# Sliding-window attention and a gated two-layer product in one program: the first batch's second half of keys and queries loaded ahead of the first layer's weights

## The chip, the cores and the metric

One core of a Trainium2 chip runs the whole program. It has five engines that run their own instruction streams in order and meet at semaphores: TensorE (PE; its weight loads are listed as PEld), VectorE (DVE), ScalarE (ACT), GpSimd (POOL) and SyncE (SP). Loads from memory are issued by POOL, since they change the type on the way (float32 in memory, 16-bit types on the chip). The metric is the device time of one execution in microseconds (us), lower is better, given as the median of several runs. Three runs of the kernel before took 290.44, 291.09 and 289.84 us.

## The reference

Two stages follow each other. First comes attention with a window of 32 positions to each side, over 8 batches, 8 heads, 576 positions and 64 channels:

```python
scores = scale * np.matmul(q, k.transpose(0, 1, 3, 2))
mask = np.abs(pos[:, None] - pos[None, :]) <= window      # window = 32
scores = np.where(mask, scores, -1000000000.0)
attn = np.exp(scores - np.max(scores, axis=-1, keepdims=True))
attn = attn / (np.sum(attn, axis=-1, keepdims=True) + 1e-09)
attn_out = np.matmul(attn, v)
```

Its output, with the heads side by side, is x (4608 tokens of 512 channels). Then come two matrix products with an activation between them:

```python
h = x @ w_in                                   # 512 -> 2048
g = h * (1.0 / (1.0 + np.exp(-1.702 * h)))
out = g @ w_out                                # 2048 -> 512
```

## The kernel before

The tokens are cut into 36 units of 128 rows (shifted by 32 rows, so that a unit's window needs its own keys and 64 of the next unit's) and into 9 tiles of 512 rows, four units each. For each unit `scores` (L238) multiplies keys and queries on PE and ACT takes the exponent; `band` (L258) multiplies by the mask on DVE; `values` (L266) multiplies by the values on PE; `norm` (L284) divides on DVE; `x_T` or `x_T2` (L298, L313) transposes the result on PE, and a copy puts it where layer one reads it. `values` needs the unit's values `ve` and a copy `vo` that is shifted by 64 rows: `odd_v(u)` (L201) copies the upper half of `ve[u]` and the lower half of `ve[u + 1]`, so it needs the loads of both.

Layer one of tile 0 is plain: `layer1_plain(0, d, half, bank)` (L378) makes two blocks of 128 features for 256 tokens with eight matrix products, and ACT applies the activation. `d` from 0 to 7 runs over the features; `d` 0 and 1 need the first quarter of w_in (`load_w1(0)`), 2 and 3 the second, and so on; `half` 0 needs units 0 and 1, `half` 1 units 2 and 3. The later tiles use a scheme with sums of blocks of w_in (`w1_sums`, L327), of w_out and of x. Layer two takes w_out in quarters (`load_w2`).

`opening` (L562) holds everything that this change touches. It is an order written out by hand, and each engine runs its share of it in this order. The staging of the first batch's keys and queries comes in two parts (`load_first`, L137, and `T_first`, L157, which transposes on PE and copies with two engines); the next tile's in one each (`load_four`, `T_four`, L173 and L181). `keep_busy` (L553) runs matrix products whose result nobody reads. Eight PSUM banks are handed out by name: A, C, B, E, LA, LB and "t", which is two. A step that takes a bank waits until the last reader of that bank is done.

POOL issues the loads one after another, in the order in which they stand. They share eight completion semaphores in turn, so a load can only be issued once the load eight places before it has landed. In the opening this is the order: first keys and queries part 0, values 0, 1, 2, first quarter of w_in, the mask, keys and queries part 1, second quarter of w_in, values 3 and 4, third quarter, the tile's keys and queries, fourth quarter, values 5 and 6, first quarter of w_out, values 7 and 8, the other quarters of w_out, and then what `fetch` brings for the later units. Unit 4's values come as two halves of 64 rows in any case, since a batch ends in the middle of it.

Of the kernel before, what the change touches and what calls it, by code (L numbers as in the profile page):

```python
# [26 lines left out]
class _Kernel:  # L27
# [166 lines left out]
    def load_v(self, u):  # L194
        if u >= self.NU:
            return
        t = self.ve[u % 9]
        for off, b, s, n in self.pieces(128 * u, 128):
            self.nc.gpsimd.dma_start(t[off:off + n, :, :self.D], self.v[b, :, s:s + n, :].rearrange("h s d -> s h d"))  # L199

    def odd_v(self, u, eng):  # L201

        vo = self.vo[u % 5]
        nxt = self.v_first if u == self.NU - 1 else self.ve[(u + 1) % 9][0:64]

        def words(ap):
            return ap.rearrange("p h d -> p (h d)").bitcast(I32)

        eng.tensor_copy(words(vo[64:128]), words(self.ve[u % 9][64:128]))  # L209
        eng.tensor_copy(words(vo[0:64]), words(nxt))  # L210
# [351 lines left out]
    def opening(self):  # L562

        nc, dve, act, pool = self.nc, self.nc.vector, self.nc.scalar, self.nc.gpsimd
        self.setup()
        dve.memset(self.idle, 0.0)
        dve.memset(self.spark, 0.0)
        for t in self.ve:
            dve.memset(t[:, :, self.D:], 1.0)
        self.load_first("k", 0)  # L570
        self.load_first("q", 0)
        make_identity(nc, self.ident)
        act.activation(self.spark, self.spark, AF.Exp)
        for u in (0, 1, 2):
            self.load_v(u)
        self.load_w1(0)
        self.setup_mask()
        self.load_first("k", 1)
        self.load_first("q", 1)
        self.cut_mask()  # L580
        self.load_w1(1)
        self.load_v(3)
        self.load_v(4)
        self.load_w1(2)
        self.load_four("k")
        self.load_four("q")
        self.load_w1(3)
        dve.tensor_copy(self.identh, self.ident)
        self.keep_busy(20, "E")
        self.T_first("k", 0, "AC", (dve, act))  # L590
        self.keep_busy(6, "E")
        self.T_first("q", 0, ("LA", "LB"), (dve, act))
        self.keep_busy(4, "E")
        for u in (5, 6):
            self.load_v(u)
        self.load_w2(0)
        for u in (7, 8):
            self.load_v(u)
        for c in (1, 2, 3):
            self.load_w2(c)  # L600
        self.load_kq("k", 8)
        self.scores(0, "t")
        self.scores(1, "AC")
        self.odd_v(0, dve)
        self.odd_v(1, dve)
        self.keep_busy(10, "E")
        self.band(0)
        self.band(1)
        self.values(0, "t")
        self.values(1, "AC")  # L610
        self.norm(0)
        self.norm(1)
        self.keep_busy(6, "E")
        self.x_T(0, "LA", act)
        self.keep_busy(4, "E")
        self.x_T(1, "LB", act)
        self.T_first("k", 1, "AC", (dve, dve))
        h, n, gelus = [], [0], []

        def l1(half, *ds):  # L620
            for d in ds:
                self.layer1_plain(0, d, half, h[n[0] % len(h)])
                n[0] += 1

        self.layer1_plain(0, 0, 0, "B", gelus)
        self.T_first("q", 1, ("LA", "LB"), (dve, act))
        self.layer1_plain(0, 1, 0, "E", gelus)
        self.odd_v(2, dve)
        self.odd_v(3, dve)
        h[:] = ["LB", "B", "E"]  # L630
        self.scores(2, "t")
        self.scores(3, "AC")
        self.layer1_plain(0, 2, 0, "LA", gelus)
        self.layer1_plain(0, 3, 0, "LB", gelus)
        self.do(gelus)
        self.band(2)
        self.band(3)
        self.values(2, "t")
        self.norm(2)
        self.values(3, "AC")  # L640
        self.norm(3)
        self.x_T2(2, "A", dve)
        l1(0, 4)
        dve.tensor_copy(self.k_first, self.kT[0][:, :, 0:64])
        dve.tensor_copy(self.v_first, self.ve[0][0:64])
        for u in (8, 9, 10, 11):
            self.fetch(u)
        l1(1, 0, 1)
        halo = self.kT[4]
        self.T_four("k", "AC", (dve, dve))  # L650
        dve.tensor_copy(self.kT[4][:, :, 0:64], halo)
        l1(1, 2, 3)
        l1(0, 5)
        self.T_four("q", "AC", (dve, act))
        l1(1, 4, 5)
        self.odd_v(4, dve)
        self.scores(4, "t")
        self.scores(5, "AC")
        for i in (3, 1, 2, 4):
            self.w1_sums((i,), 0)  # L660
        self.odd_v(5, dve)
        for d, tag in ((6, "B"), (7, "E")):
            self.layer1_plain(0, d, 0, tag, gelus)
        self.do(self.l2, 3)
        self.scores(6, "t")
        self.do(self.l2, 3)
        self.scores(7, "AC")
        self.do(gelus)
        self.do(self.l2, 2)
        self.band(4)  # L670
        self.band(5)
        self.odd_v(6, dve)
        self.odd_v(7, dve)
        self.band(6)
        self.values(4, "t")
        self.norm(4)
        self.band(7)
        self.values(5, "AC")
        self.norm(5)
        self.do(self.l2, 8)  # L680
        self.values(6, "t")
        self.norm(6)
        self.values(7, "AC")
        self.norm(7)
        h[:] = "BE"
        n[0] = 0
        for i in (3, 1):
            self.w1_sums((i,), 1)
        l1(1, 6, 7)
        self.x_T2(4, "A", act)  # L690
        self.do(self.l2, 4)
        self.x_T2(6, "t", dve)
        self.do(self.l2, 4)
# [214 lines left out]
```

## Time and profile before

| what | us |
|---|---|
| median of three runs | 290.44 |
| lowest and highest run | 289.84, 291.09 |
| span of the profiled execution, first to last instruction | 287.4 |
| what the median has beyond that span | 3.04 |
| PE busy in the span | 274.7 |
| DVE, ACT, POOL busy in the span | 216.9, 194.0, 127.3 |

The page gives the profiled execution's span and no further time for it. A row of a timeline reads: start in us from the span's start, duration in us, engine, line, operation, what is written and what is read, count, and in brackets how long the engine sat idle before it and what ended that. Rows of several equal instructions are merged. A row of the chain of waits reads: start, duration, engine or DMA, tile, line. A row of a table by stretches of time reads: the stretch, its length, the busy time of PE, PEld, DVE, ACT and POOL (instructions in brackets), the granted clock of TensorE as a share of the full one, the mean busy share of the DMA engines, and GB/s. A row of the DMA issues names what is loaded, how many such issues there are, their size as it lands, and the median time from the start of the issue to the landing.

### The profile page before, as it was taken

The numbers are of one execution on the slowest core, as the hardware profiler recorded it, in microseconds if no ns is written. First come the engines' busy times: TensorE is split into PE (matmuls) and PEld (weight loads), VectorE is DVE, ScalarE is ACT, GpSimd is POOL, SyncE is SP. The second block draws the span as 40 slices with busy tenths as digits, with TensorE's granted clock in tenths as the row PEclk, the third lists the DMA queues.
The fourth block names the chain that finished last, engine by engine and source line by source line (L and its number), as shares of the span: only waits on it lengthen the run. The fifth ranks groups of instructions, "written<-read, shape, count | busy, mean of one in ns | idle before, by whom it ended". The sixth has DMA issues, their size and how long they took to land.

```text
span 287.4 us, 9107 instructions
## 1 busy us (share of the span) xinstructions
PE 274.7 (96%) x3762; PEld 227.1 (79%) x3762; DVE 216.9 (75%) x501; ACT 194.0 (68%) x340; POOL 127.3 (44%) x192
## 2 busy tenths in 40 slices
PE   7878999999999997999999999999999999999995
PEld 5666857776777885888788888888888888888884
DVE  1756898897887975798779887988797878946731
ACT  2455784789787767676967696679668965558421
POOL 8964448798599746456345826360210000000000
PEclk9999999999999999999999999999999999999999
DMA  8999999999999999999999999998432150401023
GB/s 94 186 192 197 184 204 156 190 116 140 168 141 148 175 142 173 138 203 144 188 97 181 161 168 105 173 135 146 95 77 45 69 112 0 94 2 73 2 92 130
DMA packets 148074, 37.63 MB, mean 131 GB/s; under 512 B 134976, under 2 KB 143680, under 8 KB 148032
## 3 DMA queue, kind: packets, MB, share of 16 engines
q0 software_dynamic: 104464, 18.42, 92.3%
q1 hardware_dynamic: 43120, 18.10, 36.0%
q8 instruction: 29, 0.48, 0.7%
q10 hardware_dynamic: 448, 0.52, 0.6%
q14 instruction: 13, 0.11, 0.1%
HBM read 36.83 MB, written 9.44 MB: 161 GB/s over the span
## 4 chain that ended last, share of the span: by engine, by line
PE 81%; DMA 5%; DVE 5%; ACT 3%; POOL 2%; issue 2%; DVEq 0%; ACTq 0%; POOLq 0%
PE h L70 38%; PE o L70 34%; PE pv L70 3%; DMA xT<-x 3%; PE sc L70 2%; DMA kq<-in_k_dram 2%; DVE x L294 2%; ACT p L256 1%; PE tp L322 1%; POOL ve L199 1%; ACT L256 1%; DVE p L264 1%; PE tp L189 1%; PE tp L232 1%; ACT g L419 1%
## 5 line engine op out<-in xcount | busy, mean ns | idle before, releaser
L419 ACT ACTIVATE g<-h 128x512 f16<-128x512 f32 x128 | 72.1, 598 | 35.8 <-PE h L70 35.0
L70 PEld LDWEIGHTS <-g 128*128 128x128 f16 x576 | 54.4, 98 | 11.4 <-issue 1.8
L70 PEld LDWEIGHTS <-a 128*128 128x128 f16 x512 | 49.1, 97 | 12.7 <-DVE xs L354 2.1
L70 PE MATMUL h<-xs,a 128*128 128x256 f16 x384 | 57.6, 272 | 1.2 <-DVE xs L354 0.9
L70 PE MATMUL o<-w,g 128*128 128x256 f16 (+1 forms) x320 | 55.3, 294 | 0.9 <-issue 0.8
L70 PEld LDWEIGHTS <-w 128*128 128x128 f16 x512 | 49.1, 98 | 7.8 <-issue 1.2
L70 PE MATMUL h<-xT,w 128*128 128x256 f16 x384 | 54.0, 273 | 1.1 <-issue 1.0
L199 POOL DMA_DIRECT2D ve<-in_v_dram x40 | 34.0, 855 | 40.7 <-issue 33.7
L70 PEld LDWEIGHTS <-gs 128*128 128x128 f16 x384 | 36.8, 98 | 5.2 <-issue 0.4
L256 ACT ACTIVATE p<-sc 128x512 bf16<-128x512 f32 x72 | 36.6, 619 | 3.2 <-PE sc L70 3.2
L70 PE MATMUL o<-b,gs 128*128 128x256 f16 x256 | 37.8, 273 | 1.0 <-issue 0.5
L70 PE MATMUL o<-b,g 128*128 128x256 f16 x256 | 37.3, 273 | 0.0
L432 DVE TENSOR_TENSOR h<-h,s 128x512 f32<-128x512 f32 x32 | 22.3, 698 | 18.2 <-PE h L70 18.2
L131 POOL DMA_DIRECT2D qst<-in_q_dram x35 | 28.1, 805 | 5.5 <-DMA w<-in_moe_w_out_dram 3.2
L131 POOL DMA_DIRECT2D kst<-in_k_dram x31 | 26.4, 854 | 8.5 <-DMA ve<-in_v_dram 2.6
L67 ACT COPY h<-h 128x512 f32<-128x512 f32 x32 | 18.6, 581 | 16.6 <-PE h L70 16.2
L294 DVE TENSOR_TENSOR x<-pv,rec 128x256 f16<-128x256 f32 (+1 forms) x53 | 27.6, 520 | 1.8
L438 DVE TENSOR_TENSOR h<-h,s 128x512 f32<-128x512 f32 x32 | 22.4, 700 | 5.1 <-PE h L70 4.6
L264 DVE TENSOR_TENSOR p<-p,mask 128x1024 bf16<-128x1024 bf16 x36 | 24.6, 685 | 0.9 <-ACT p L256 0.8
L209 POOL COPY vo<-ve 64x264 int32<-64x264 int32 x28 | 13.4, 480 | 24.9 <-PE pv L70 23.8
L67 ACT COPY s<-h 128x512 f32<-128x512 f32 x32 | 19.1, 596 | 3.0 <-PE h L70 1.8
L70 PE MATMUL h<-xs,w 128*128 128x256 f16 x128 | 19.2, 273 | 0.0
(85 smaller groups left out, 361.1 us busy)
## 6 DMA issues: line engine op xcount, KB each, us to landing
out_dram<-o_sb SPq DMA_DIRECT2D x33, 256.0 KB, 3.9
ve<-in_v_dram POOLq DMA_DIRECT2D x32, 128.0 KB, 6.3
kst<-in_k_dram POOLq DMA_DIRECT2D x25, 128.0 KB, 6.8
qst<-in_q_dram POOLq DMA_DIRECT2D x21, 128.0 KB, 6.1
w<-in_moe_w_in_dram POOLq DMA_DIRECT2D x4, 512.0 KB, 8.9
w<-in_moe_w_out_dram POOLq DMA_DIRECT2D x4, 512.0 KB, 13.4
qst<-in_q_dram POOLq DMA_DIRECT2D x7, 96.0 KB, 5.5
kq<-in_q_dram POOLq DMA_DIRECT2D x2, 256.0 KB, 5.9
```

Source lines behind the costliest of these rows:

```text
L67: (eng.copy if eng is self.nc.scalar else eng.tensor_copy)(out, in_)
L70: self.nc.tensor.matmul(out, lhsT, rhs, start=start, stop=stop, skip_group_check=True)
L131: self.nc.gpsimd.dma_start(t[off:off + n], src[b, :, s:s + n, :].rearrange("h s d -> s h d"))
L189: self.nc.tensor.transpose(tp[64 * (h % 2):64 * (h % 2) + 64, h // 2, j, :], src[:, 4 * i + h, j, :], self.ident)
L199: self.nc.gpsimd.dma_start(t[off:off + n, :, :self.D], self.v[b, :, s:s + n, :].rearrange("h s d -> s h d"))
L209: eng.tensor_copy(words(vo[64:128]), words(self.ve[u % 9][64:128]))
L256: self.nc.scalar.activation(p[:, eo].rearrange("k h s -> k (h s)"), sc[eo], AF.Exp, scale=self.scale)
L264: (eng or self.nc.vector).tensor_mul(pv, pv, msk.to_broadcast([128, 8, 2, SQ]))
L294: dve.tensor_mul(x[:, 4 * at:4 * (at + n), :].rearrange("p (b h) d -> p b h d", b=n), acc[:, :, :, :D], r.to_broadcast([128, n, 4, D]))
L419: act.activation(g[:, f, 256 * half:256 * half + 256], bank.rearrange("p (i n) -> p i n", i=2), AF.Gelu_apprx_sigmoid)
L432: dve.tensor_add(e, b, s7)
L438: dve.tensor_add(c, b, s7)
```

## The change

Only `opening` changes, and one helper is new. The helper `load_v_part(lo, n)` loads n rows of the values from row lo on; a unit's values can so be loaded in two halves.

- Loads. The mask is set up right after values 0 and 1. Then come the first half of values 2, keys and queries part 1, and only then the first quarter of w_in, the second half of values 2, values 3, the first half of values 4, the second and third quarter of w_in, the tile's keys and queries, the fourth quarter, the first quarter of w_out, the second half of values 4, values 5 and 6, the second quarter of w_out, values 7 and 8, and the rest.
- `odd_v(3)` runs on POOL instead of DVE, between the tile's queries and the fourth quarter of w_in.
- Keys part 1 are transposed between `values(0)` and `values(1)`, and queries part 1 right after; their four copies are all on ACT. x of units 0 and 1 goes through one `x_T2` with a copy on DVE instead of two `x_T` on ACT. `scores(2)` and `scores(3)` follow at once, ahead of layer one.
- Layer one of tile 0 begins with `d` 0 and 1; then units 2 and 3 are finished; then come (half 0: 2, 3), (half 1: 0, 1), (half 1: 2, 3), (half 0: 4, 5), the transposes of the tile's keys, (half 1: 4, 5) and the transposes of the tile's queries. x of units 2 and 3 goes through two `x_T`, with a copy on ACT and one on DVE.
- The four `w1_sums` of half 0 stand ahead of the copies of the tile's keys instead of behind `scores(5)`.
- Ten of the unread matrix products go, four come.

```diff
+    def load_v_part(self, lo, n):
+        u, at = divmod(lo, 128)
+        t = self.ve[u % 9]
+        for off, b, s, m in self.pieces(lo, n):
+            self.nc.gpsimd.dma_start(t[at + off:at + off + m, :, :self.D],
+                                     self.v[b, :, s:s + m, :].rearrange("h s d -> s h d"))
...
-        for u in (0, 1, 2):
-            self.load_v(u)
-        self.load_w1(0)
+        self.load_v(0)
+        self.load_v(1)
         self.setup_mask()
+        self.load_v_part(256, 64)
         self.load_first("k", 1)
         self.load_first("q", 1)
         self.cut_mask()
+        self.load_w1(0)
+        self.load_v_part(320, 64)
+        self.load_v(3)
+        self.load_v_part(512, 64)
         self.load_w1(1)
-        self.load_v(3)
-        self.load_v(4)
         self.load_w1(2)
         self.load_four("k")
         self.load_four("q")
+        self.odd_v(3, pool)
         self.load_w1(3)
+        self.load_w2(0)
+        self.load_v_part(576, 64)
+        self.load_v(5)
+        self.load_v(6)
+        self.load_w2(1)
+        self.load_v(7)
+        self.load_v(8)
+        self.load_w2(2)
+        self.load_w2(3)
+        self.load_kq("k", 8)
...
-        for u in (5, 6):
-            self.load_v(u)
-        self.load_w2(0)
-        for u in (7, 8):
-            self.load_v(u)
-        for c in (1, 2, 3):
-            self.load_w2(c)
-        self.load_kq("k", 8)
...
         self.values(0, "t")
+        self.T_first("k", 1, "BE", (act, act))
         self.values(1, "AC")
         self.norm(0)
         self.norm(1)
-        self.keep_busy(6, "E")
-        self.x_T(0, "LA", act)
-        self.keep_busy(4, "E")
-        self.x_T(1, "LB", act)
-        self.T_first("k", 1, "AC", (dve, dve))
+        self.T_first("q", 1, ("LA", "LB"), (act, act))
+        self.x_T2(0, "t", dve)
+        self.scores(2, "BE")
+        self.scores(3, ("LA", "LB"))
...
-        self.layer1_plain(0, 0, 0, "B", gelus)
-        self.T_first("q", 1, ("LA", "LB"), (dve, act))
-        self.layer1_plain(0, 1, 0, "E", gelus)
+        self.layer1_plain(0, 0, 0, "A")
+        self.layer1_plain(0, 1, 0, "C")
+        self.band(2)
         self.odd_v(2, dve)
-        self.odd_v(3, dve)
-        h[:] = ["LB", "B", "E"]
-        self.scores(2, "t")
-        self.scores(3, "AC")
-        self.layer1_plain(0, 2, 0, "LA", gelus)
-        self.layer1_plain(0, 3, 0, "LB", gelus)
-        self.do(gelus)
-        self.band(2)
         self.band(3)
         self.values(2, "t")
+        self.values(3, "BE")
         self.norm(2)
-        self.values(3, "AC")
         self.norm(3)
-        self.x_T2(2, "A", dve)
-        l1(0, 4)
+        self.keep_busy(4, "LB")
+        self.x_T(2, "LA", act)
+        self.x_T(3, "LB", dve)
+        h[:] = ["B", "E", "A", "C", "LA", "LB"]
+        l1(0, 2, 3)
+        l1(1, 0, 1)
         dve.tensor_copy(self.k_first, self.kT[0][:, :, 0:64])
         dve.tensor_copy(self.v_first, self.ve[0][0:64])
+        for i in (3, 1, 2, 4):
+            self.w1_sums((i,), 0)
         for u in (8, 9, 10, 11):
             self.fetch(u)
-        l1(1, 0, 1)
+        l1(1, 2, 3)
+        l1(0, 4, 5)
         halo = self.kT[4]
         self.T_four("k", "AC", (dve, dve))
         dve.tensor_copy(self.kT[4][:, :, 0:64], halo)
-        l1(1, 2, 3)
-        l1(0, 5)
-        self.T_four("q", "AC", (dve, act))
         l1(1, 4, 5)
+        self.T_four("q", "BE", (dve, act))
         self.odd_v(4, dve)
         self.scores(4, "t")
         self.scores(5, "AC")
-        for i in (3, 1, 2, 4):
-            self.w1_sums((i,), 0)
         self.odd_v(5, dve)
```

From `odd_v(5)` on the order of every engine is as before.

## The prediction

> **What bounds the kernel now.** I read the head of the page, then the table by stretches, then the chain of waits.
>
> ```profile
> span 287.4 us, 9107 instructions
> PE 274.7 (96%) x3762; PEld 227.1 (79%) x3762; DVE 216.9 (75%) x501; ACT 194.0 (68%) x340; POOL 127.3 (44%) x192
> L209 POOL COPY vo<-ve 64x264 int32<-64x264 int32 x28 | 13.4, 480 | 24.9 <-PE pv L70 23.8
> ```
>
> ```profile
> 20.22:24.43 4.21, 2.00 (x44) 1.36 (x43) 3.90 (x10) 3.80 (x6) 3.24 (x4) 1.00 1.39 198
> 36.30:43.50 7.20, 6.67 (x132) 3.50 (x131) 6.80 (x19) 6.04 (x11) 3.21 (x4) 1.00 1.32 203
> 53.40:287.40 234.00, 227.38 (x2968) 191.99 (x2967) 180.64 (x413) 163.15 (x291) 91.19 (x135) 1.00 1.23 121
> ```
>
> PE is the bound over the span, and from 53.4 us on (97% busy) the work and its order stay as they are. So what the change is worth is decided in the first 43.5 us, and then shifts all that follows. There PE is short of work at 20.22 to 24.43 (2.00 of 4.21 us). At 36.3 to 43.5 it looks filled, but DVE (6.80 of 7.20) sets the pace:
>
> ```profile
> 28.38 2.73 PE h L70 x24
> ...
> 36.44 1.58 ACT p L256 x3
> ...
> 38.05 0.69 DVE p L264
> ...
> 39.74 0.29 DVE vo L210
> ...
> 40.03 0.60 DVE p L264
> ...
> 42.75 0.43 DVE x L294
> ...
> 43.54 1.85 PE h L70 x16
> ```
>
> The chain runs from ACT's exponents of units 4 and 5 to `band(5)` (38.05), the four copies of `odd_v(6)` and `odd_v(7)` (the last at 39.74, over by 40.03), `band(6)`, the norms, and back to PE at 43.5. What stands before that, and what PE still has to do behind it, is the same work in both kernels. The shift of the end is therefore the shift of 40.03.
>
> **Loads, where the time is decided.** Issues on POOL, and how long each took to land:
>
> ```profile
> 3.37 2.67 POOL L199 DMA_DIRECT2D ve<-in_v_dram  x3
> 6.75 0.36 POOL L102 MEMSET mask<- 128x256 bf16 x1
> 8.47 0.76 POOL L143 DMA_DIRECT2D kq<-in_k_dram  x1
> 9.22 0.76 POOL L143 DMA_DIRECT2D kq<-in_q_dram  x1
> 26.49 0.87 POOL L199 DMA_DIRECT2D ve<-in_v_dram  x1 [2.31 <-DMA o_sb<-in_k_dram]
> 27.38 0.76 POOL L119 DMA_DIRECT2D w<-in_moe_w_out_dram  x1
> ```
>
> ```profile
> kq<-in_k_dram POOLq DMA_DIRECT2D x1, 320.0 KB, 4.5
> kq<-in_q_dram POOLq DMA_DIRECT2D x1, 256.0 KB, 5.0
> ...
> kq<-in_k_dram POOLq DMA_DIRECT2D x1, 256.0 KB, 6.3
> kq<-in_q_dram POOLq DMA_DIRECT2D x1, 256.0 KB, 6.9
> ...
> ve<-in_v_dram POOLq DMA_DIRECT2D x1, 128.0 KB, 10.4
> w<-in_moe_w_out_dram POOLq DMA_DIRECT2D x1, 512.0 KB, 12.0
> ```
>
> Keys part 1 land at 8.47 + 6.3 = 14.8, queries part 1 at 9.22 + 6.9 = 16.1, values 8 at 26.49 + 10.4 = 36.9, the second quarter of w_out at 27.38 + 12.0 = 39.4. So that quarter costs 2.5 us of the queue; a unit's values cost about 0.89 (2.67 for three). The table shows 198 and 203 GB/s: the queue is full, and a reordering moves landings against each other but doesn't bring the whole set in earlier.
>
> After: the mask takes 6.75 to 8.47, 1.72 us, and now stands at 5.15, behind values 0 and 1. The half of values 2 is issued at 6.87 (0.7, estimated between a half and a whole of 0.89), keys part 1 at 7.57, queries part 1 at 8.33. Their landing is not shown for this order. From below: with little ahead of them they take as long as the first pair, 4.5 and 5.0: 12.1 and 13.3. From above: 6.3 and 6.9 again: 13.9 and 15.2. A third way checks it: the bytes up to the queries are those that were in at 16.1, less a quarter of w_in (2.5) and half a unit (0.45), so 13.2 if the queue never runs dry. I take 12.1 and 13.3, which is 0.1 of lost queue time; the upper end is 2.0. Behind them in turn: w_in's first quarter 15.8, the half of values 2 at 16.3, values 3 at 17.2, half of values 4 at 17.6.
>
> The other end of the queue costs. Values 7 and 8 now stand behind w_out's second quarter. Up to values 8 the set is exactly the one that was in at 39.4, so values 8 land at 39.4 + 0.1 = 39.5 instead of 36.9. The last copy of `odd_v(7)` waits for them, and on DVE everything named above is queued behind it.
>
> **Compute, step by step**, with these rows:
>
> ```profile
> 16.48 0.71 PE L168 MATMUL tp<-ident,kq 64*64 64x64 bf16 x32
> 17.24 0.59 ACT L67 COPY kq<-tp 128x512 bf16<-128x512 bf16 x1 [2.29 <-PE tp L168]
> 18.60 2.07 ACT L256 ACTIVATE p<-sc 128x512 bf16<-128x512 f32 x4 [0.78 <-PE sc L70]
> 22.28 0.21 DVE L293 RECIPROCAL rec<-pv 128x8 f32<-128x8 f32 x1
> 23.89 0.42 DVE L294 TENSOR_TENSOR x<-pv,rec 128x256 f16<-128x256 f32 x1
> 27.98 2.36 DVE L67 COPY kq<-tp 128x1024 bf16<-128x1024 bf16 x2 [2.26 <-PE tp L189]
> 31.04 1.11 PE L189 MATMUL tp<-ident,o_sb 128*64 128x128 bf16 x32
> 32.19 1.01 ACT L67 COPY kq<-tp 128x1024 bf16<-128x1024 bf16 x1 [0.45 <-PE tp L189]
> 33.93 0.70 PE L70 MATMUL sc<-kq 64*64 64x64 bf16 x48
> 34.65 1.28 ACT L256 ACT_TABLE_LOAD   x1
> 35.95 4.03 ACT L256 ACTIVATE p<-sc 128x512 bf16<-128x512 f32 x8
> ```
>
> Keys: transposed by 12.8, two ACT copies by 13.6. Queries: transposed by 14.0, copies (0.59 each) by 14.85. `scores(2)` and `(3)` take 0.70, to 15.55; the exponents 2.07, to 17.3 (before they began at 18.60, so 3.3 us are won here). Two tiles of layer one wait for w_in: 15.8 to 17.6 (16 products at 2.73 / 24 = 0.114). DVE: `band(2)` to 17.0, `odd_v(2)` waits for values 3 and ends at 17.8, `band(3)` 18.45. `odd_v(3)` is on POOL now, two copies of 0.48 from 17.6 to 18.55; it holds up `values(3)` by 0.1. Behind it on POOL stands w_in's fourth quarter, and behind that every later load; the queue then has the third quarter and the next tile's keys and queries still to move, so this costs nothing. Without that cover it would be the 0.96. `values(3)` is done by 18.9, the two norms take 23.89 + 0.42 - 22.28 = 2.03 from 18.45 to 20.5, `x_T(3)` ends at 20.9. Here most of the 3.3 us has gone into a wait for DVE.
>
> From there PE has 64 products (7.3) to 28.2 and `T_four` of the keys (1.11) to 29.3. Its copies on DVE (1.18 each) run from half of it, 28.75, to 29.95 and 31.1. Layer one's next two tiles take banks A and C, which these copies still read; before, they took other banks. So they end at 32.0 instead of 31.1: 0.9 of new wait. `T_four` of the queries ends at 33.1, ACT's copy (1.01) at 34.15. Before, two tiles of layer one covered that copy; now `scores(4)` stands right behind it, at 34.15 against 33.93. But ACT has no activation left in between: its table load (1.28) starts at 34.15 instead of 34.65. The compute chain is 0.5 us earlier at the exponents, and, without any wait for values, at the end of `odd_v(7)`: 39.5 instead of 40.03. `w1_sums` move from 33.8 on DVE into idle DVE time ahead of 28.75, at nothing: the exponents, not DVE, released `band(5)`. The junk products that go (a net six) ended in a wait for DVE in any case. Copies that change between ACT and DVE before 21 us are in the steps above.
>
> **The sum.** Compute alone: -0.5. Values 8: 39.5 + 0.29 = 39.8 against 40.03: -0.25. The later of the two holds: **-0.25 us**, so 290.44 - 0.25 = **290.2 us**. The profiled execution would go from 287.4 to 287.15; the median has 3.04 beyond the span, which I leave as it is. The forecast is no change that can be told.
>
> **Rivals.**
> 1. *The queue runs dry, and the kernel is slower.* Before, 512 KB of w_in were queued ahead of the mask's 1.72 us and fed the queue through it. Now POOL makes the mask with only keys, queries and values 0 and 1 issued, and all that follows in a full queue is late by what is lost. For it: keys part 1 were never seen to land faster than 6.3 us after their issue. Against it: these 6.3 had w_in ahead of them. Price: up to 2.0 lost, so values 8 at 41.4, the copy over at 41.7, +1.65: 292.1. It is slower than before from 0.35 us lost on.
> 2. *Values 8 are not that late, and compute sets the end.* Their landing lies between 36.9, where it was, and 39.5. Then -0.5, 289.9; if layer one also does not wait on A and C (0.9, since `T_four` copies may start earlier), -1.4, 289.0. For it: the queue mixes loads, a later one can overtake in part. Against: 198 to 203 GB/s leave no room.
> 3. *TensorE's clock falls.* PE has about 2.2 us of work between 17.6 and 20.9, with four junk products. The row at 20.22 shows 2.00 busy of 4.21 at a granted clock of 1.00, which speaks against it. If the clock halved for the next two groups of 16 products, they would cost 3.65 more, less 0.25: 293.6.
>
> The Trainium skill (TensorE: Matmul & The Clock Gate, Part 1: The HAM clock gate) says that the clock halves after an idle window of about 3.4 us. By that rule removing junk products is a risk; the trace agrees only that a gap of some 2 us costs no clock, and shows no longer one.
>
> 4. *The change doesn't do what it says*: `scores(2)` and `(3)` don't move forward because queries part 1 land no earlier. That is the upper end of rival 1.
>
> **Chances.** Forecast, within half a microsecond of 290.2: 0.47. Rival 1: 0.30. Rival 2: 0.19. Rival 3: 0.04. About 0.5% (1.45 us: 289.0 and 291.9) is what a measurement of this kernel can tell from no change; the three runs lie 1.25 apart. Rival 1 has its price just above that bound, and I put 0.22 of its 0.30 there; of rival 2, 0.15 below 289.0, since its best end lies there and runs scatter; rival 3 all above. Faster 0.15, same 0.59, slower 0.26. The range goes from rival 2's 289.0 to rival 1's 292.1, widened by half the scatter: 288.7 to 292.6. The forecast's own: 289.6 to 291.
>
> **What would show it.** Queries part 1 landing at 13.3 and values 8 at 39.5; `scores(2)` near 14.9; exponents of unit 4 from 35.45; DVE waiting for values ahead of `odd_v(7)`, with its last copy over at 39.8. I am wrong if DVE doesn't wait there, if w_in's first quarter lands after 17 us, or if anything past 53 us takes another time than before.

## The result, and the profile after

The changed kernel takes 291.98 us (median of 20 runs, 288.96 to 294.58); the kernel before, run beside it on the same chip, takes 289.41 (20 runs, 287.32 to 292.14). The ratio is 1.0078, with a 95% interval of 1.0052 to 1.0104: slower by about 2.3 us (0.0078 times 289.41; the two medians lie 2.57 apart). The forecast was 290.2 and no change that can be told. So the time lies inside the range that was given, but the forecast took the wrong case; the first rival, a queue that runs dry, is what happened.

The profiled execution of the changed kernel took 290.17 us, 1.7 beyond its span. Head of its page, and the shares of the chain that ended last:

```profile
span 288.5 us, 9098 instructions
PE 276.7 (96%) x3756; PEld 228.4 (79%) x3756; DVE 216.7 (75%) x497; ACT 195.2 (68%) x342; POOL 129.1 (45%) x195
PE 76%; DMA 14%; DVE 3%; POOL 3%; ACT 2%; issue 2%; DVEq 0%; POOLq 0%
```

Busy sums and instruction counts hardly differ from before. The chain itself does. Its longest pieces in order of time (start, duration, what), changed kernel:

```profile
9.33 8.32 DMA w<-in_moe_w_in_dram
17.94 12.40 DMA o_sb<-in_q_dram
31.11 10.69 DMA ve<-in_v_dram
46.00 1.85 PE h L70 x16
```

The first 42 us are now issues on POOL and three transfers that wait for one another: w_in's first quarter lands at 9.33 + 8.32 = 17.65 and frees the completion semaphore that the tile's queries need; these land at 30.34 and free the one for values 8, which land at 31.11 + 10.69 = 41.80. DVE's timeline shows who waits for them:

```profile
40.17 0.29 DVE L216 COPY vo<-ve 64x264 int32<-64x264 int32 x1
40.99 0.34 DVE L217 COPY vo<-ve 64x264 int32<-64x264 int32 x1 [0.52 <-DMA ve<-in_v_dram]
41.36 0.30 DVE L216 COPY vo<-ve 64x264 int32<-64x264 int32 x1
41.82 0.68 DVE L217 COPY vo<-ve 64x264 int32<-64x264 int32 x1 [0.17 <-DMA ve<-in_v_dram]
42.42 0.67 DVE L271 TENSOR_TENSOR p<-p,mask 128x1024 bf16<-128x1024 bf16 x1
```

These are the four copies of `odd_v(6)` and `odd_v(7)`, then `band(6)`. Two of the copies wait for a landing, and the last is over at 42.50; before it was over at 40.03. PE's next group of layer one follows 2.46 later as well (46.00, before 43.54). That is the loss, and it is made before 43 us. The late queue reaches it by a second way too: layer one waits for w_in, and the exponents of unit 4 begin 1.40 later (37.35, before 35.95; 36.24 in experiment 1 below, where w_in is in time):

```profile
17.70 1.92 PE L70 MATMUL h<-xT,w 128*128 128x256 f16 x16 [0.57 <-DMA w<-in_moe_w_in_dram]
```

```profile
37.35 2.06 ACT L263 ACTIVATE p<-sc 128x512 bf16<-128x512 f32 x4
```

Where the loss begins is seen on the queue. POOL's timeline, changed kernel:

```profile
5.12 0.34 POOL L102 MEMSET mask<- 128x256 bf16 x1
5.53 1.33 POOL L105 TENSOR_SCALAR_AFFINE_SELECT mask<-mask 64x128 bf16<-64x128 bf16 x4
6.82 0.69 POOL L205 DMA_DIRECT2D ve<-in_v_dram  x1
7.49 0.69 POOL L143 DMA_DIRECT2D kq<-in_k_dram  x1
8.16 0.70 POOL L143 DMA_DIRECT2D kq<-in_q_dram  x1
```

Between 5.12 and 6.82 POOL makes the mask and issues nothing. Two microseconds later that shows in what the queue moves. The table by stretches (last column: GB/s), of the kernel before and then of the changed one:

```profile
8.00:10.00 2.00, 2.00 (x67) 1.63 (x61) 1.51 (x4) 1.34 (x3) 1.93 (x5) 1.00 1.90 169
10.00:12.00 2.00, 1.10 (x22) 0.67 (x20) 1.60 (x4) 1.31 (x3) 1.91 (x6) 1.00 1.27 207
12.00:14.00 2.00, 1.91 (x32) 1.65 (x32) 1.88 (x7) 0.44 (x1) 2.00 (x4) 1.00 1.43 193
```

```profile
8.00:10.00 2.00, 2.00 (x38) 1.40 (x37) 0.76 (x2) 0.31 (x1) 1.91 (x7) 1.00 1.19 82
10.00:12.00 2.00, 2.00 (x59) 1.47 (x58) 1.20 (x4) 1.25 (x4) 2.00 (x4) 1.00 1.31 177
12.00:14.00 2.00, 1.46 (x54) 1.08 (x52) 1.54 (x4) 1.25 (x4) 2.00 (x4) 1.00 1.13 140
```

Before: (169 + 207 + 193) times 2 us, 1138 KB. After: (82 + 177 + 140) times 2, 798 KB. The 340 KB that are missing are 1.7 us at the some 200 GB/s of a full queue. The traces of all experiments agree: in the same six microseconds the five traces with this opening order of the loads move 798 to 872 KB, and the seven in which a quarter of w_in is issued ahead of the mask move 1138 to 1172 KB.

Not all of the 2.46 us is left at the end of this one execution: its span is only 1.1 longer. Part comes back at a transposing transfer of x near 104 us. The chains of before and after there:

```profile
103.43 8.78 DMA xT<-x
...
113.91 1.05 PE h L70 x8
```

```profile
104.61 8.83 DMA xT<-x
...
115.14 1.05 PE h L70 x8
```

In both kernels the chain goes through this transfer; it starts 1.18 later instead of 2.46, and PE behind it is 1.23 late. The ratio over all runs gives 2.3 us all the same. Whether other executions regain as much is not shown, since only one of each kernel has a trace.

### The profile page after: what moved, and what is told of

It is laid out like the page before. It is cut to its first block, busy times and chain, and to the rows that moved or that the text cites. A ratio compares the mean times of both kernels' runs of the same rounds, so it can differ in the third digit from the quotient of the medians.

```text
span 288.5 us, 9098 instructions
## 1 busy us (share of the span) xinstructions
PE 276.7 (96%) x3756; PEld 228.4 (79%) x3756; DVE 216.7 (75%) x497; ACT 195.2 (68%) x342; POOL 129.1 (45%) x195
## 4 chain that ended last, share of the span: by engine, by line
PE 76%; DMA 14%; DVE 3%; POOL 3%; ACT 2%; issue 2%; DVEq 0%; POOLq 0%
PE o L70 35%; PE h L70 34%; DMA o_sb<-in_q_dram 4%; DMA ve<-in_v_dram 4%; PE pv L70 3%; DMA xT<-x 3%; DMA w<-in_moe_w_in_dram 3%; PE sc L70 2%; DVE x L301 1%; ACT p L263 1%; POOL kq L143 1%; PE tp L239 1%; PE tp L329 1%; POOL ve L199 1%; ACT g L426 1%
## 5 line engine op out<-in xcount | busy, mean ns | idle before, releaser
L199 POOL DMA_DIRECT2D ve<-in_v_dram x37 | 32.0, 866 | 42.1 <-issue 27.8
L439 DVE TENSOR_TENSOR h<-h,s 128x512 f32<-128x512 f32 x32 | 22.3, 698 | 17.9 <-PE h L70 17.6
L216 POOL COPY vo<-ve 64x264 int32<-64x264 int32 x29 | 14.6, 504 | 25.8 <-PE pv L70 24.5
```

The costliest lines, as they stand in the source:

```text
L439: dve.tensor_add(e, b, s7)
```

## The experiments

Three theories were held against each other. D: the queue runs dry while POOL makes the mask. O: only the new place of values 7 and 8, behind w_out's second quarter, costs. C: the new order of compute costs (the bank wait among it). All ratios are to the kernel before, run on the same chip.

**1. The mask later.** The changed kernel with the mask behind the issue of w_in's first quarter:

```diff
-        self.setup_mask()
         self.load_v_part(256, 64)
         self.load_first("k", 1)
         self.load_first("q", 1)
-        self.cut_mask()
         self.load_w1(0)
+        self.setup_mask()
+        self.cut_mask()
```

> The changed kernel with the mask made behind the first quarter of w_in instead of behind values 1; the order of the loads is kept. Theory D (the load queue runs dry between 8 and 14 us, because POOL makes the mask for 1.7 us with little queued): the queue carries over 180 GB/s from 8 us on, queries part 1 land by 13.3 us, the first quarter of w_in by 16, values 8 by 40.2 instead of 41.8, and the ratio to the kernel before falls from 1.008 to between 0.998 and 1.003. Rival O (values 7 and 8 stand behind the second quarter of w_out, that alone costs): values 8 still land after 41, ratio above 1.005. Rival C (the new order of the computation costs, by its waits for banks A and C and for odd_v(3) on POOL): ratio above 1.005 whenever the loads land.

Measured: 289.48 us, ratio 1.0013 (0.9985 to 1.0041). The stretches, and DVE's copies of `odd_v(7)`:

```profile
8.00:10.00 2.00, 2.00 (x64) 1.65 (x60) 1.64 (x4) 1.40 (x3) 1.71 (x8) 1.00 1.82 182
10.00:12.00 2.00, 1.47 (x53) 1.12 (x51) 1.70 (x4) 1.25 (x3) 1.95 (x6) 1.00 1.38 201
12.00:14.00 2.00, 0.99 (x44) 0.79 (x40) 1.45 (x5) 1.07 (x2) 2.00 (x4) 1.00 1.28 203
```

```profile
39.71 0.57 DVE L216 COPY vo<-ve 64x264 int32<-64x264 int32 x1
40.31 0.29 DVE L217 COPY vo<-ve 64x264 int32<-64x264 int32 x1
```

The same instructions in another order, and the queue moves 1172 KB in these six microseconds, no less than the 1138 of the kernel before. The first quarter of w_in lands at 15.5 instead of 17.65 and values 8 at 39.6 instead of 41.80. No copy waits for a landing. The change's loss of 2.3 us shrinks to 0.4 (0.0013 times 289.48), and the two intervals don't overlap. That is the cause, shown by taking it away. It also rules out O and C as the whole cause, since the place of values 7 and 8 and the order of compute are those of the changed kernel. It also shows how compute alone stands: the last copy is over at 40.60, 0.57 later than before, not 0.5 earlier.

**2. Values 7 and 8 ahead of w_out's second quarter**, in the changed kernel:

```diff
-        self.load_w2(1)
         self.load_v(7)
         self.load_v(8)
+        self.load_w2(1)
```

> The changed kernel with values 7 and 8 loaded ahead of the second quarter of w_out, as before. D: the 2 us lost early stay; values 8 land near 39.3, DVE no longer waits for them ahead of odd_v(7), and band(5), which is 1.4 us late in the changed kernel, sets the end: ratio 1.004 to 1.006. O: ratio 0.998 to 1.001, no slower than before. C: 1.006 to 1.008, as the changed kernel.

Measured: 291.26, ratio 1.0086 (1.0047 to 1.0125). DVE no longer waits for values 8 (in at 39.4), and yet nothing is won that the ratio could tell; D had 1.004 to 1.006. The second way stays: w_in is late, and the exponents with it. In the profiled execution TensorE's clock fell as well, which is told under the hardware below, so its trace doesn't show how late they would be without that. The five runs with a mean granted clock of 0.999 or more have a median of 290.67; of the runs of the kernel before beside them, 14 have that clock, with a median of 288.93, and of the changed kernel's runs 7, with 291.99. So a part may be won, but most of the loss stays, and O falls as the whole cause. Experiment 6 shows the rest: with the mask late, the place of values 7 and 8 makes no difference that can be told.

**3 and 4. One half of the change each.** The changed kernel's compute with the order of loads of before (`odd_v(3)` on POOL kept), and the compute of before with the changed order of loads (`odd_v(3)` on DVE, as before). Of the first, the head of the difference to the changed kernel:

```diff
-        self.load_v(0)
-        self.load_v(1)
+        for u in (0, 1, 2):
+            self.load_v(u)
+        self.load_w1(0)
         self.setup_mask()
-        self.load_v_part(256, 64)
         self.load_first("k", 1)
...
```

> The new order of the computation with the loads in the order of the kernel before. D: nothing is lost in the queue and values 8 land at 37, but queries part 1 come at 16.1 instead of 14.9, so that scores(2) begin near 17.4 instead of 16.1 and the exponents of unit 4 near 38.5: ratio 1.006 to 1.010. O: ratio at most 1.001, since values 8 are early. C: ratio above 1.005, with waits for banks A and C of 0.9 us and more in front of layer one.

> The old order of the computation with the loads in the new order. D: values 8 land near 41.8 as in the changed kernel and DVE waits for them ahead of odd_v(7): ratio 1.007 to 1.010. O: the same. C: ratio at most 1.003, since the old computation has none of the new waits.

Measured: the first 291.74, ratio 1.009 (1.0049 to 1.0132, nine runs); the second 293.52, ratio 1.015 (1.0102 to 1.0198, six runs). Neither half alone is better than both together, so the change can't be split into a part that gains and one that loses; the first can't be told from the changed kernel's 1.0078. In the first, the queue loses nothing (1152 KB from 8 to 14 us), but PE stands for keys part 1, which land late in that order, ahead of `values(1)`:

```profile
14.64 1.09 PE L168 MATMUL tp<-ident,kq 64*64 64x64 bf16 x32 [2.64 <-DMA kq<-in_k_dram]
```

Its ratio fits D's number and C's alike; only O's (at most 1.001) falls. The second lies outside all three numbers. C, which had at most 1.003, falls as the whole cause. D's sign fails too: values 8 land at 42.3, but DVE reaches the copies of `odd_v(7)` only at 43.31 and doesn't wait. What is late there is compute: layer one still runs ahead of units 2 and 3 and w_in comes later, so that ACT's exponents of unit 2 begin at 22.19, before at 18.60. Both ratios hold a loss of clock besides: in both traces the granted clock falls to 0.50, and 8 of the 9 and 5 of the 6 runs have a mean of 0.994 or less.

**5. The suspected cost doubled.** The changed kernel with the set-up of the mask made twice:

```diff
         self.setup_mask()
+        self.setup_mask()
```

> The changed kernel with the mask's set-up made twice on POOL, at the place of the change, same values: the suspected cost doubled (1.7 us more of POOL ahead of the half of values 2). D: the load queue stays short of work for about as much longer, values 8 land near 43.5 instead of 41.8, and the ratio to the kernel before goes from 1.008 to between 1.012 and 1.016. C: POOL's set-up is not on the path; ratio 1.007 to 1.010.

Measured: 291.91, ratio 1.0102 (1.0043 to 1.0161), six runs. The first quarter of w_in lands at 18.7, 1.05 after the changed kernel's. Values 8 are issued at 32.48 and land 10.7 later, at 43.2, 1.4 after the changed kernel's. The queue:

```profile
8.00:10.00 2.00, 2.00 (x85) 1.66 (x79) 1.67 (x4) 0.99 (x2) 1.94 (x5) 1.00 0.41 32
10.00:12.00 2.00, 1.00 (x10) 0.65 (x7) 0.58 (x3) 1.66 (x4) 1.91 (x7) 1.00 1.13 84
```

The hole in the queue is deeper and longer, as D says: from 8 to 14 us it moves 592 KB, below all other traces. The landing of values 8 is the weaker sign, since experiment 9 has the same 43.2 with the mask made once. The ratio's interval holds numbers of both theories, and five of the six runs had a lowered clock, so the time of this run decides nothing.

**6. Both repairs**, the mask of experiment 1 and the place of values 7 and 8 of experiment 2.

> Mask behind the first quarter of w_in, and values 7 and 8 ahead of the second quarter of w_out. D: with the queue fed, values 8 (39.6 with the mask late alone) land near 37.2; the order at the tail is worth at most 0.3 us more, as the exponents of unit 4 start at 36.2 in any case: ratio 0.998 to 1.002. O: clearly faster than with the mask late alone, ratio 0.994 to 0.997. C: as the changed kernel, above 1.005.

Measured: 289.74, ratio 1.0036 (1.0000 to 1.0072), between the theories' numbers; the interval reaches down into D's, and excludes O's. The last copy of `odd_v(7)` is over at 40.60 as in experiment 1, with values 8 in by some 37 us: compute sets the end, and an earlier landing is worth nothing.

**7 and 8. The wait for banks.** `T_four` of the keys in banks LA and LB instead of A and C, so that layer one's next tiles don't wait for its copies: once on top of both repairs, once on the changed kernel alone.

```diff
-        self.T_four("k", "AC", (dve, dve))
+        self.T_four("k", ("LA", "LB"), (dve, dve))
```

> The same, and T_four of the keys in banks LA and LB instead of A and C, so that layer one's next tiles don't wait for its copies on DVE. D, with the bank wait of 0.9 us last once the loads are in time: exponents of unit 4 from 35.4, ratio 0.994 to 0.999. If the bank wait is hidden by something else: 0.998 to 1.002.

> The changed kernel with T_four of the keys in banks LA and LB, nothing else. D: the wait in front of layer one goes (0.9 us), but values 8 still land at 41.8 and DVE waits for them: ratio 1.006 to 1.009. C: the bank wait is part of the loss: ratio 1.003 to 1.006.

With the repairs: 288.23, ratio 0.9981 (0.9950 to 1.0012). PE's first group behind the transposes with the repairs alone, and with the banks as well:

```profile
30.70 2.17 PE L70 MATMUL h<-xT,w 128*128 128x256 f16 x16 [0.87 <-DVE kq L67]
```

```profile
30.47 1.92 PE L70 MATMUL h<-xT,w 128*128 128x256 f16 x16
```

The wait of 0.87 is gone, and `band(6)` begins at 39.80 instead of 40.53. Without the repairs: 291.96, ratio 1.0101 (1.0061 to 1.0140), a little above what was expected. ACT's exponents of unit 4 come 1.67 earlier (35.68, in the changed kernel 37.35), 0.87 of it by the bank's wait and some 0.5 because layer one's 64 products already began earlier in this execution (22.23, in the changed kernel 22.72). All of it goes into a longer wait for the same landings:

```profile
41.34 0.34 DVE L217 COPY vo<-ve 64x264 int32<-64x264 int32 x1 [1.19 <-DMA ve<-in_v_dram]
41.71 0.29 DVE L216 COPY vo<-ve 64x264 int32<-64x264 int32 x1
42.21 0.63 DVE L217 COPY vo<-ve 64x264 int32<-64x264 int32 x1 [0.21 <-DMA ve<-in_v_dram]
```

This pair shows that the landing of values 7 and 8 bounds the changed kernel: a compute path that is 1.67 shorter at the exponents gains nothing while the landings stand (values 8 at 42.2). That the time came out above the expected 1.006 to 1.009 has a likely reason in the clock: PE stands still from 42.35 to 44.34 in this trace, the granted clock falls to 0.50 at 47, and 9 of the 12 runs had a lowered clock.

**9. `odd_v(3)` back on DVE** in the changed kernel:

```diff
-        self.odd_v(3, pool)
...
         self.odd_v(2, dve)
+        self.odd_v(3, dve)
```

> The changed kernel with odd_v(3) back on DVE (behind odd_v(2)), so that POOL copies nothing between its issues. D (the queue is already late by some 1.8 us from the mask, and the copies on POOL stand while the queue still has two quarters of w_in and the tile's keys and queries to move): values 8 land at 41.0 to 42.0 as in the changed kernel, ratio to the kernel before 1.005 to 1.010. Rival P (POOL's copies hold the queue up as well): values 8 land by 40.5 or earlier, ratio 1.003 or less.

Measured: 291.66, ratio 1.0070 (1.0030 to 1.0109); values 8 issued at 32.61, in 10.6 later at 43.2, later than either theory had it. No further time of the queue is lost: from 8 to 30 us it moves 178 GB/s in both traces. The bytes come in another order. The first quarter of w_in, issued at 9.33 in both, lands at 18.47 instead of 17.65, and the tile's keys, issued at 13.9 in both, at 29.8 instead of 27.6, while w_in's fourth quarter, without the copies ahead of it, is issued 0.9 earlier. What decides that order stays open. POOL's copies are not what holds the queue up: without them the time is the same.

**10 and 11. What is left on the chain.** On top of experiment 7: `T_four` of the queries ahead of layer one's tiles (half 1: 4, 5), so that these cover its copies; and then `odd_v(6)` ahead of `band(4)`, where DVE idled.

```diff
+        h[:] = "BE"
+        n[0] = 0
...
+        self.T_four("q", "AC", (dve, act))
         l1(1, 4, 5)
-        self.T_four("q", "BE", (dve, act))
...
+        self.odd_v(6, dve)
         self.band(4)
         self.band(5)
-        self.odd_v(6, dve)
```

> The variant with the mask late, values 7 and 8 early and T_four of the keys in banks LA and LB, and in addition T_four of the queries in A and C ahead of layer one's tiles (half 1: 4, 5), which go to B and E. If what is left on the chain are the copies of the tile's queries with nothing to cover them: ACT's exponents of unit 4 begin at 35.2 instead of 35.80, band(6) at 39.2 instead of 39.80, time 0.6 us below that variant, ratio to the kernel before 0.995 to 0.998. If not (the table load or the activations come later by as much): exponents at 35.8, ratio 0.998 to 1.001.

> As the variant with the covered copies, and odd_v(6) on DVE ahead of band(4) instead of behind band(5). If DVE idles ahead of band(4) as it did (0.85 us) and values 7 are in by 36.5: band(6) begins 0.6 us earlier than without it, at 38.6, ratio to the kernel before 0.993 to 0.996. If the copies wait for values 7: band(4) and band(6) stay or come later, ratio as without it or above.

Measured: 288.34, ratio 0.9983 (0.9946 to 1.0020) for the first, not below experiment 7; the ratio fits both of its numbers, and its trace neither (the exponents begin at 34.34, `band(6)` at 38.71). **287.45, ratio 0.9934 (0.9902 to 0.9966)** was measured for the two together: faster than the kernel before by about 1.9 us (0.0066 times 289.38), and than the changed one by about 4 (by the two ratios, 1.0078 and 0.9934). ACT's and DVE's rows of the last variant:

```profile
35.25 4.39 ACT L263 ACTIVATE p<-sc 128x512 bf16<-128x512 f32 x8
```

```profile
36.03 0.29 DVE L217 COPY vo<-ve 64x264 int32<-64x264 int32 x1
36.44 0.69 DVE L271 TENSOR_TENSOR p<-p,mask 128x1024 bf16<-128x1024 bf16 x1
...
38.61 0.68 DVE L271 TENSOR_TENSOR p<-p,mask 128x1024 bf16<-128x1024 bf16 x1
```

The exponents begin at 35.25 (35.2 expected), `odd_v(6)` is over before `band(4)`, and `band(6)` begins at 38.61 (38.6 expected). That both agree is in part luck: this execution began slowly (see the hardware below), and PE's 64 products of layer one start 0.9 later in it than in the trace of the first (22.36 against 21.46). It took 288.90, 1.45 more than the median. So the whole set, early keys and queries with the five repairs, is faster than the kernel before. What the repairs would be worth on the kernel before wasn't run.

## Why the prediction was wrong, point by point

- **What bounds the kernel, and by how much the end shifts: right.** The end was said to shift with the end of DVE's last copy of `odd_v(7)`. That copy is 2.47 later and PE's next group 2.46. That nothing past 53 us takes another time was not right for the profiled pair (1.2 us of the delay is regained near 104 us); the ratio over all runs shows the full loss. The sum also started from 290.44, the median of three runs, where 20 runs give 289.41; and the 3.04 beyond the span belongs to two executions, since each run lies some 1.7 beyond its own span. The size of the loss doesn't hang on that, but how close the times came does: rival 1's 292.1 meets the measured 291.98 because a base that is 1.0 too high makes up for a loss put too low, and that the time lies inside the range is luck of the same kind.
- **The landings in the new order: the step that failed.** "I take 12.1 and 13.3, which is 0.1 of lost queue time; the upper end is 2.0." The lost queue time is the term that was mis-sized. Shown: 1.7 us by the bytes of 8 to 14 us, and 1.85 more than forecast by the landing of w_in's first quarter (17.65 instead of 15.8), near the end that was not taken. Keys part 1, issued at 7.49, land at 12.5 (12.1 forecast), and queries part 1 are in at 14.9 (13.3 forecast), where the transposes that waited for them begin. The changed kernel's rows for the queries:

```profile
14.93 0.71 PE L168 MATMUL tp<-ident,kq 64*64 64x64 bf16 x32 [0.37 <-DMA kq<-in_q_dram]
...
16.12 1.00 PE L70 MATMUL sc<-kq 64*64 64x64 bf16 x48
```

  In the four other traces with this opening order the queries land at 13.4 to 14.3, nearer the forecast, and w_in's first quarter all the same at 17.6 to 18.5. So the queries' landing was no measure of what the queue loses behind them. The value taken came from "a third way" that counts bytes and holds only "if the queue never runs dry". That was the very question. The rows to decide it stood in the prediction: POOL's 1.72 us on the mask, with values 1 the last thing issued ahead of it. Before, a quarter of w_in (2.5 us of the queue) was issued just ahead of the mask and covered it; with that cover gone the cost is about the mask's own length. Experiment 1 puts the cover back and the loss goes away with the hole; experiment 5 doubles the mask and the hole grows.
- **Values 8 late, DVE waits for them: right in mechanism, wrong in size.** They were put at 39.5 and landed at 41.80; the copy was put at 39.8 and ended at 42.50. Rival 1 had 41.4, 41.7 and +1.65 and is the case that came true, with 0.4 us too little for the landing and 0.8 for the copy and the shift (+2.47).
- **Compute at -0.5: wrong as well.** Without the hole in the queue (experiment 1) the last copy is over at 40.60, 1.1 later than the 39.5 that the steps gave, though `scores(2)` began at 14.95 (14.85 forecast). The bank wait was right (0.9, shown 0.87). What was too short lies before and behind it: the transposes of the keys begin at 28.69 instead of 28.2, the 16 products behind the wait take 2.17 instead of 16 times 0.114, and one copy of `odd_v(7)` takes 0.57 instead of 0.29.
- **Rival 2** (values 8 are in early, compute sets the end) came true only in the variants with the mask late, and there at +0.57, not -0.5. **Rival 4**: `scores(2)` and its exponents did move forward (16.90, before 18.60), so the change did what it says.
- **Rival 3**, the clock: not the cause. In the changed kernel's profiled execution the granted clock stays at 1.00 in all stretches shown, and the loss is there in runs at the full clock too, as told below. Two things in this part of the prediction were wrong. The row of 20.22 to 24.43 was read as a gap of some 2 us at the full clock; the idle time in it comes in pieces of 1.02 and 1.08 and some shorter ones, and the trace has no gap of PE behind its first 5 us that is longer than 1.08. And its price counts the -0.25 twice: 290.44 - 0.25 + 3.65 is 293.8, not 293.6.
- **The range**: half of the 1.25 by which the three runs differ is 0.6, which gives 288.4 to 292.7 instead of 288.7 to 292.6. Nothing hangs on it.

## What to carry to other kernels

- When a compute step on the engine that issues the loads is moved, look at how many microseconds of transfers stand issued ahead of it: if that is less than the step's length, what is missing is lost for every load behind it, however full the queue is later. Here 1.7 us of mask behind small loads cost about 2 us; behind the issue of a 512 KB load it cost nothing that could be told.
- A sum over bytes of a full queue is an upper bound on its speed, and can't be used to check whether the queue is full.
- When two paths end close together (here a landing and a chain of compute), repairing one can show nothing until the other is repaired too, as the banks did in experiments 8 and 7; test repairs together before dropping one.

## What the runs showed of the hardware

TensorE's clock fell after a gap as long as one that the prediction held to be harmless ("a gap of some 2 us costs no clock"). In experiment 2's profiled execution PE has nothing to do from 10.61 to 12.66. The table by stretches (stretch, length, PE's busy time; the granted clock stands third from the end):

```profile
10.61:12.66 2.05, 0.00 (x2) 0.00 (x1) 1.11 (x3) 0.67 (x2) 2.05 (x4) 1.00 1.50 180
14.00:15.00 1.00, 1.00 (x46) 0.92 (x39) 0.93 (x5) 1.00 (x3) 1.00 (x3) 0.93 1.15 184
15.00:20.00 5.00, 3.60 (x64) 2.58 (x63) 2.85 (x6) 3.99 (x7) 2.08 (x3) 0.50 1.63 184
```

Some 2 us after that gap the clock is halved, up to 21.7, and 16 products of layer one take 3.59 us instead of 1.92:

```profile
18.09 3.59 PE L70 MATMUL h<-xT,w 128*128 128x256 f16 x16 [1.40 <-DMA w<-in_moe_w_in_dram]
```

A gap of the same length cost nothing in experiment 8's trace (first row); a second one there was followed by the halved clock (second and third row):

```profile
15.57:17.61 2.04, 0.01 (x2) 0.01 (x1) 0.69 (x1) 2.02 (x5) 0.00 (x0) 1.00 1.97 167
42.35:44.34 1.99, 0.00 (x0) 0.00 (x1) 1.96 (x5) 0.16 (x1) 1.28 (x2) 1.00 1.33 198
47.25:50.50 3.25, 3.25 (x19) 2.31 (x18) 1.84 (x5) 1.66 (x3) 2.62 (x4) 0.50 2.24 147
```

Between 10 and 60 us the clock falls in five of the 13 traces, those of experiments 2, 3, 4, 5 and 8. In each of these PE has a gap of 1.6 to 2.7 us shortly before or at the fall; in the others no gap is longer than 1.1, but for experiment 9's of 1.72, after which the clock stays. The Trainium skill (TensorE: Matmul & The Clock Gate, Part 1: The HAM clock gate) has the clock halve after an idle window of about 3.4 us that runs freely. In experiment 2 only 2.05 us of idleness came before it, with work that was not dense around it, so a gap below that figure is not safe. Why a gap of some 2 us costs the clock in one place and not in another, the runs don't settle.

The kernel before loses clock in some of its runs, too: in the 29 beside experiments 9 to 11 the mean granted clock is 0.998 or more in 16 (median 288.60 us) and lower in 13 (median 290.56). Of the changed kernel's 20 runs 9 are at 0.998 or more (median 291.25) and 11 lower (292.23). So the slowdown is there at the full clock too. What a lowered clock goes with differs from kernel to kernel: 2.0 us in the kernel before, 1.0 in the changed one, 0.1 in experiment 1.

One row of the trace doesn't fit the clock's column. Up to about 10.5 us PE is slower in the changed kernel's profiled execution (the 32 transposes of the queries' part 0 take 1.09 us, in the kernel before 0.71) though the granted clock reads 1.00 in both; experiments 7, 9 and 11 have the same; in the others it is over by some 7 us. Its cause is not shown. The loss doesn't come from it: w_in's first quarter lands at 17.6 to 18.0 in experiments 2, 4 and 8 too, which have the same opening order and don't begin slowly.
